# Scores of two attention items in one block of every second slot, with the product with v between their main parts

## The chip, the cores and the metric

The kernel runs on one core of a Trainium2 chip. A core has five engines that run side by side, each in its own order: TensorE (PE, with its weight loads PEld), VectorE (DVE), ScalarE (ACT), GpSimd (POOL) and SyncE (SP). The metric is the device time of one execution in microseconds (us), the median of three runs.

## The reference

Attention that keeps the 32 largest scores of each row, and then a two-layer MLP with an exact GELU on its output:

```python
batch, n_heads, seq, head_dim = (8, 8, 576, 64)
scores = (1/sqrt(D)) * (q @ k.T)                 # per batch and head
kth    = np.partition(scores, -32)[..., -32]     # 32nd largest of each row
scores = np.where(scores >= kth, scores, -1e9)
attn   = exp(scores - max); attn = attn / (sum(attn) + 1e-9)
out    = attn @ v
x = out.transpose(0, 2, 1, 3).reshape(4608, 512)
g = gelu(x @ w_in)                               # w_in 512 x 2048
return g @ w_out                                 # w_out 2048 x 512
```

Everything is in fp32. Each fp32 matmul is two passes on TensorE, so the profile counts two for each one in the code; its transposes are one pass.

## The kernel before

*Items.* Two heads make a pair (four pairs in a batch, 32 in all). An item is 128 rows of the score matrix for both heads of a pair, 2 x 576 columns in an SBUF tile `s` of which there are five. A main item `(pair, t)` with t from 0 to 3 is one block of 128 query rows. The last 64 rows of four heads (two pairs) are packed into one last item, t = 4 (`NM`). There are 144 items: in a batch 16 main ones, which go through the pairs with t even and odd next to each other, and two last ones. In batches of even number the last items come behind the main ones, in those of odd number ahead of them, so that four last items stand side by side in every 36.

*Slots.* The order of every engine is written out by hand in one loop over slots n (148 of them, some 10 to 12 us each). Slot n works on several items at once: scores of item n+2 (`scores`, TensorE and ScalarE), top 32 of item n (`top_k`, VectorE), softmax of item n-1 (ScalarE, in two halves), normalising of item n-1 (`normalise`, two GpSimd multiplies of 1.72 us), transposes of the probabilities of item n-2 (`transposes`: `tails`, which writes `tp_t`, and two of `main`, which write `tp`), and the product with v for item n-3 (`attend`, tile `o`). A product is made only for main items of odd t, for both row blocks at once, and for every last item. Main items of odd t have odd numbers, so products of main items fall into even slots; those of last items fall into two even and two odd slots.

*Scores.* The scores against the last 64 keys and against the first 512 are made apart. The last keys (`t_ps`, L280) use the full array, 128 rows of which half hold zeros in the keys' block, or 64-column tiles for last items (L294). The main scores (`s_ps`, L284, L305) use half the array's rows for each of the two heads, so that two matmuls run at once. The product with v (L448, L459) uses half the array's columns for each head. `s_ps` takes two PSUM banks and has one buffer; `t_ps`, `o`, `tp_t`, `tp` and the transposed q and k (`tp_qk`, L239) share the tag `tp` with two. ScalarE copies both parts of the scores into `s` and scales them (L288, L289).

*MLP.* Between the steps of a slot stand pieces of the MLP, one by one (`mlp(1)`): eight pieces a slot, each two matmuls or so of the first layer (`h_ps`, L500) or the second (`y_ps`, L536), as soon as their tokens are done. ScalarE's GELUs (L511) are issued in pairs at a few places (`run_gelus`), most of them at the end of a slot, and each pair costs a table load (L511) and one back to exp (L371).

*Who waits for whom.* Within a slot ScalarE's second softmax half stands behind the copies of `tp_t` and of the first `tp`. It gives the denominator (`den`, GpSimd L363), then VectorE's reciprocal (`rden`, L357), which stands behind the last max of `top_k(n)`, then GpSimd's `threshold(n)` (`neg`, `bias`) and the two multiplies of `normalise(n-1)` (L382). In the next slot TensorE's `tp_t` (L399, L404) waits for those multiplies.

The order around the scores in a slot is this:

```python
scores(n + 2)
product = attend(n - 3)
late = n > START
mlp(1)
tr = transposes(n - 2)
...
softmax(n - 1, 0)
mlp(1)
```

Where no MLP piece can go on before the product of this slot, `tp_t` is issued directly behind the product, and the tokens are set free at that place.

Of the kernel before, what the change touches and what calls it, by code (L numbers as in the profile page):

```python
# [14 lines left out]
def kernel(  # L15
# [19 lines left out]
    nc = tc.nc  # L35
    f32, i32, u32 = mybir.dt.float32, mybir.dt.int32, mybir.dt.uint32
    bf16, i16, u16 = mybir.dt.bfloat16, mybir.dt.int16, mybir.dt.uint16
    AF = mybir.ActivationFunctionType
    ALU = mybir.AluOpType

    B, H, S, D = q.shape
    P = 128
# [4 lines left out]
    NM = S // P  # L47
    SM = NM * P
    TL = S - SM
# [6 lines left out]
    scale = 1.0 / float(D) ** 0.5  # L56
# [4 lines left out]
    work = ctx.enter_context(tc.tile_pool(name="work", bufs=2))  # L61
    ps = ctx.enter_context(tc.tile_pool(name="ps", bufs=2, space=bass.MemoryType.PSUM))
# [21 lines left out]
    def raw_of(n, pair):  # L84
        return raws[n][pair % len(raws[n])]
# [120 lines left out]
    items, starts = [], []  # L206
# [14 lines left out]
    N = len(items)  # L221


    KT = SM + 2 * P
    qk_of = {}
# [26 lines left out]
    S_of, stat_of = {}, {}  # L252

    def row(i, e):
        return S_of[i][:, e * S : (e + 1) * S]

    def spread(t, step, n):

        return bass.AP(tensor=t.tensor, offset=t.offset, ap=[list(t.ap[0]), [step, 2], [1, n]])

    def half(r, e):


        return slice((r ^ e) * TL, ((r ^ e) + 1) * TL)
# [2 lines left out]

        return spread(t[:, e * TL :], step + (TL if e == 0 else -TL), TL)

    def scores(i):  # L270
        if i >= N:
            return
        pair, t = items[i]
        S_of[i] = s = work.tile([P, 2 * S], f32, tag="s", bufs=5, name="s")
        s_ps = ps.tile([P, 2, 512], f32, tag="s", bufs=1, name="s_ps")
        t_ps = ps.tile([P, 512], f32, tag="tp", name="t_ps")
        if t < NM:
            qk = qk_of[pair]
            lhsT = qk[:, t * P : (t + 1) * P]
            nc.tensor.matmul(t_ps[:, 0:P], lhsT=lhsT, rhs=qk[:, SM + P : KT], start=True, stop=True)  # L280
            for c in range(2):
                for e in range(2):
                    rows = slice(e * D, (e + 1) * D)
                    nc.tensor.matmul(  # L284
                        s_ps[:, e, c * 256 : (c + 1) * 256], lhsT=lhsT[rows, :],
                        rhs=qk[rows, KT + c * 256 : KT + (c + 1) * 256], start=True, stop=True,
                    )
            nc.scalar.activation(spread(s, S + TL, SM), s_ps, func=AF.Copy, scale=scale)  # L288
            nc.scalar.activation(s[:, SM : S + TL], t_ps[:, 0:P], func=AF.Copy, scale=scale)  # L289
        else:  # L290
            for r in range(2):
                qk = qk_of[pair + r]
                for e in range(2):
                    nc.tensor.matmul(  # L294
                        t_ps[half(r, e), r * TL : (r + 1) * TL],
                        lhsT=qk[:, SM + e * TL : SM + (e + 1) * TL],
                        rhs=qk[:, SM + P + e * TL : SM + P + (e + 1) * TL],
                        start=True, stop=True,
                    )

            for r in range(2):
                qk = qk_of[pair + r]
                for e in range(2):
                    rows = slice(e * D, (e + 1) * D)
                    nc.tensor.matmul(  # L305
                        s_ps[half(r, e), r, :], lhsT=qk[rows, SM + e * TL : SM + (e + 1) * TL],
                        rhs=qk[rows, KT:], start=True, stop=True,
                    )
            s2 = s.rearrange("p (r n) -> p r n", r=2)
            nc.scalar.activation(s2[:, :, 0:SM], s_ps, func=AF.Copy, scale=scale)  # L310
            nc.scalar.activation(
                s2[:, :, SM:S], t_ps[:, 0:P].rearrange("p (r n) -> p r n", r=2),
                func=AF.Copy, scale=scale,
            )

    def top_k(i, hooks):

# [47 lines left out]
    def softmax(i, e):  # L365

        if i < 0 or i >= N:
            return
        st, s = stat_of[i], row(i, e)
        nc.scalar.activation(s, s, func=AF.Prelu, bias=st["neg"][:, e, 1:2], scale=1.0, alpha=STEEP)  # L370
        nc.scalar.activation(  # L371
            s, s, func=AF.Exp, bias=st["bias"][:, e : e + 1], scale=1.0,
            accum_out=st["den"][:, e : e + 1],
        )
# [13 lines left out]
    def transposes(i):  # L388
# [36 lines left out]

        return [tails] + [lambda e=e: main(e) for e in range(2)]

    n_tok, read = [0], [0]

    def attend(i):  # L430

        if i < 0 or i >= N:
            return False
        pair, t = items[i]
        b, at = divmod(pair, NP)
        if t < NM and t % 2 == 0:
            return False
        pt = pt_now[0]
        o = ps.tile([P, 512], f32, tag="tp", name="o")
        n, row = (2 * P, (t - 1) * P) if t < NM else (TL, SM)  # L440
        tok = place_of(b, row)
        assert read[0] >= tok + n - RING
        c = slice(tok % RING, tok % RING + n)
        if t < NM:
            vt = raw_of("v", pair)
            for j in range(NJ):
                for e in range(2):
                    nc.tensor.matmul(  # L448
                        o[e * D : (e + 1) * D, 0:n], lhsT=vt[:, j, e, :],
                        rhs=pt[:, e * NM + j if j < NM else 2 * NM, :],  # L450
                        start=(j == 0), stop=(j == NJ - 1),
                    )
            nc.scalar.copy(out=xT[:, at, c], in_=o[:, 0:n])
        else:
            for r in range(2):
                vt = raw_of("v", pair + r)
                for j in range(NJ):
                    for e in range(2):
                        nc.tensor.matmul(  # L459
                            o[e * D : (e + 1) * D, r * TL : (r + 1) * TL], lhsT=vt[:, j, e, :],  # L460
                            rhs=pt[:, r, j, half(r, e)], start=(j == 0), stop=(j == NJ - 1),
                        )
            nc.scalar.copy(
                out=xT[:, at : at + 2, c],
                in_=o[:, 0 : 2 * TL].rearrange("p (r n) -> p r n", r=2),
            )

        if t == (NM if b % 2 == 0 else NM - 1):
            for r in range(2 if t == NM else 1):
                load("v", pair + r + NP + 1)  # L470
        if at == (NP - 1 if t < NM else NP - 2):
            assert n_tok[0] == tok
            n_tok[0] = tok + n
        return True

# [98 lines left out]
    def mlp(n):  # L576
        for _ in range(n):
            if done[0] >= len(pieces) or pieces[done[0]][0] > ready[0] or left[0] == 0:
                return
            pieces[done[0]][1]()  # L580
            done[0] += 1
            left[0] -= 1
# [18 lines left out]
    for pair in range(2):  # L601
        for piece in transpose_qk(pair, pair == 0):
            piece()
        if pair == 0:
            scores(0)
            scores(1)

# [6 lines left out]
    for pair in range(2, n_pairs):  # L616
        b, p = divmod(pair, NP)
# [3 lines left out]
    for n in range(ahead):  # L621

        left[0] = 7 if START < n < START + 2 * NP else 8
        weights_add(unit_in(n))
        scores(n + 2)
        product = attend(n - 3)
        late = n > START
        mlp(1)
        tr = transposes(n - 2)
        if product and n > START and done[0] < len(pieces) and pieces[done[0]][0] > ready[0]:  # L630

            for piece in tr[:1]:
                piece()
            tr, ready[0] = tr[1:], n_tok[0]
        softmax(n - 1, 0)
        mlp(1)
        if not late:
            softmax(n - 1, 1)
        mlp(1)
        prep = prep_in.pop(n, [])  # L640
        if len(prep) > 1 and len(tr) == 3:
            tr, prep = tr[:1] + prep[:1] + tr[1:], prep[1:]
        for piece in tr[:-1]:
            piece()
            ready[0] = n_tok[0]
            mlp(1)
        ready[0] = n_tok[0]
        if late:
            softmax(n - 1, 1)
        add_small(n - 1)  # L650
        for piece in tr[-1:] + prep:
            piece()
            mlp(1)

        run_gelus()
        mlp(left[0])
        run_gelus()
        if n < N:
            top_k(n, {3: lambda: inverse(n - 1)})
        else:  # L660
            inverse(n - 1)
        threshold(n)
        normalise(n - 1)

        weights_sign(unit_in(n))
        weights_size(unit_in(n + 1))
        if n >= FIRST:
            load_weights(n + 2)
        if n <= NP:
            load("v", n)  # L670
# [38 lines left out]
```

## Time and profile before

| | |
|---|---|
| median of 3 runs | 1660.15 us (1660.02 to 1661.66) |
| span in the profile | 1658.1 us |
| PE, DVE, ACT, POOL busy | 96%, 86%, 71%, 40% |
| scores of last keys, L280: passes, mean | 256, 289 ns |
| main scores, L284: passes, mean | 1024, 417 ns (pairs run at once) |
| product with v, L448: passes, mean | 1280, 389 ns (pairs run at once) |
| copy of the main scores, L288 | 128 x 1027 ns |
| copy of the last keys' scores, L289 | 128 x 277 ns |
| POOL multiply, L382 | 288 x 1723 ns |

A mean duration of a matmul is from its start to its modelled end, and matmuls overlap; what a block costs is read from the start of one block to the start of the next. The waits in the trace are listed by who waited for whom. PE's longest are `tp_t` for POOL (40.2 us in 11 places, nearly all of it in the first 160 us), and ACT's are for `s_ps` (144.8 us in 79 places) and `tp` (103.4 us in 121), which says that ACT is mostly ahead of PE at these places.

### The profile page before, as it was taken

How to read it: one execution, taken by the hardware profiler on the slowest of the kernel's cores; microseconds unless marked ns; L12 is line 12 of the kernel's file. 1: busy time of each engine (PE TensorE's matmuls, PEld its weight loads, DVE VectorE, ACT ScalarE, POOL GpSimd, SP SyncE). 2: the span in 40 equal slices, each digit the busy share in tenths (PEclk: the TensorE clock that was granted, in tenths of full speed). 3: DMA queues.
4: the chain of work that ended last, by engine and by line, in shares of the span. 5: the costliest groups of instructions: out<-in, count | busy, mean ns of one | idle time of the engine just before them, and what ended most of it. 6: DMA issues, size and time to landing. Idle time of an engine off the chain costs nothing.

```text
span 1658.1 us, 25071 instructions
## 1 busy us (share of the span) xinstructions
PE 1590.1 (96%) x8832; PEld 1079.1 (65%) x8832; DVE 1428.5 (86%) x3043; ACT 1182.8 (71%) x2131; POOL 661.6 (40%) x761
## 2 busy tenths in 40 slices
PE   6559999999999999999999999999999999999999
PEld 4336566766666667676666667676666666666665
DVE  7999899998999898998999888998889898999800
ACT  6888777777777777777777777777777777777720
POOL 3769653333333333333333333333333333333300
PEclk7779999999999999999999999999999999999999
DMA  6422210011100111001110111001110001000000
GB/s 162 138 99 97 84 49 1 14 29 29 37 14 22 29 30 35 1 28 36 29 28 1 43 29 43 1 14 28 44 35 1 27 15 32 5 14 3 5 13 13
DMA packets 126621, 56.14 MB, mean 34 GB/s; under 512 B 117760, under 2 KB 117792, under 8 KB 126496
## 3 DMA queue, kind: packets, MB, share of 16 engines
q1 hardware_dynamic: 125376, 54.25, 12.2%
q8 instruction: 70, 1.15, 0.3%
q14 instruction: 55, 0.45, 0.1%
q10 hardware_dynamic: 1056, 0.26, 0.1%
q0 software_dynamic: 64, 0.03, 0.0%
HBM read 45.08 MB, written 9.44 MB: 33 GB/s over the span
## 4 chain that ended last, share of the span: by engine, by line
PE 89%; DVE 6%; ACT 2%; POOL 1%; issue 1%; POOLq 0%; ACTq 0%
PE h_ps L500 30%; PE y_ps L536 29%; PE o L448 8%; PE s_ps L284 7%; PE tp L417 7%; DVE top L331 3%; DVE rest L334 3%; PE tp_qk L239 2%; PE t_ps L280 2%; PE o L459 1%; PE tp_t L399 1%; PE s_ps L305 1%; POOL s L382 1%; DVE w_in_sb L199 0%; ACT s L371 0%
## 5 line engine op out<-in xcount | busy, mean ns | idle before, releaser
L331 DVE MAX8 top<-rest 128x8 f32<-128x576 f32 x864 | 609.9, 748 | 0.0
L500 PE MATMUL h_ps<-xT,w_in_sb 128*128 128x256 f32 (+1 forms) x2560 | 554.5, 361 | 3.7 <-ACT g L511 3.7
L536 PE MATMUL y_ps<-w_out_sb,g 128*128 128x512 f32 x1152 | 549.4, 599 | 0.0
L382 POOL TENSOR_SCALAR s<-s,rden 128x576 f32<-128x576 f32 x288 | 493.5, 1723 | 1.0 <-issue 0.7
L500 PEld LDWEIGHTS h_ps<-xT,w_in_sb 128*128 128x128 f32 x2560 | 429.2, 191 | 66.7 <-issue 16.8
L334 DVE MATCH_REPLACE8 rest<-top,rest 128x576 f32<-128x576 f32 x576 | 423.7, 744 | 0.0
L363 POOL TENSOR_SCALAR den<-den 128x2 f32<-128x2 f32 x144 | 32.0, 222 | 831.7 <-ACT s L371 830.7
L536 PEld LDWEIGHTS y_ps<-w_out_sb,g 128*128 128x128 f32 x1152 | 195.0, 190 | 166.4 <-issue 164.3
L288 ACT ACTIVATE s<-s_ps 128x1024 f32<-128x1024 f32 x128 | 131.5, 1027 | 166.5 <-PE s_ps L284 144.8
L371 ACT ACTIVATE s<-s,bias 128x576 f32<-128x576 f32 x288 | 223.3, 775 | 13.0 <-ACT s L370 0.4
L370 ACT ACTIVATE s<-s,neg 128x576 f32<-128x576 f32 x288 | 224.0, 778 | 0.5 <-POOL neg L346 0.4
L424 ACT COPY pt<-tp 128x512 f32<-128x512 f32 x256 | 147.1, 575 | 103.6 <-PE tp L417 103.4
L334 DVE MATCH_REPLACE8 rest<-top,s 128x576 f32<-128x576 f32 x288 | 211.9, 744 | 0.0
L417 PEld LDWEIGHTS tp<-ident,s 128*128 128x128 f32 x1152 | 147.9, 145 | 89.3 <-issue 59.2
L331 DVE MAX8 top<-s 128x8 f32<-128x576 f32 x288 | 201.9, 743 | 3.9 <-ACT s L289 3.9
L417 PE MATMUL tp<-ident,s 128*128 128x128 f32 x1152 | 177.9, 279 | 4.3 <-ACT pt L400 4.2
L448 PE MATMUL o<-pt,raw_v 128*64 128x256 f32 x1280 | 155.1, 389 | 0.0
L284 PE MATMUL s_ps<-qk 64*128 64x256 f32 x1024 | 151.8, 417 | 0.7 <-ACT s L288 0.7
L357 DVE RECIPROCAL rden<-den 128x2 f32<-128x2 f32 x144 | 23.2, 161 | 139.9 <-POOL den L363 139.3
L448 PEld LDWEIGHTS o<-pt,raw_v 128*64 128x64 f32 x1280 | 87.5, 139 | 65.8 <-issue 23.9
L284 PEld LDWEIGHTS s_ps<-qk 64*128 64x128 f32 x1024 | 91.8, 194 | 23.7 <-issue 1.8
L511 ACT ACTIVATE g<-h_ps 128x512 f32<-128x512 f32 x144 | 78.6, 595 | 34.0 <-PE h_ps L500 33.2
(63 smaller groups left out, 1070.2 us busy)
## 6 DMA issues: line engine op xcount, KB each, us to landing
raw_q<-in_q_dram SPq DMA_DIRECT2D x64, 128.0 KB, 2.3
raw_v<-in_v_dram SPq DMA_DIRECT2D x64, 128.0 KB, 2.4
out_dram<-y SPq DMA_DIRECT2D x32, 256.0 KB, 2.1
w_out_sb<-in_moe_w_in_dram SPq DMA_DIRECT2D x16, 511.8 KB, 4.8
raw_k<-in_k_dram SPq DMA_DIRECT2D x62, 128.0 KB, 2.4
w_out_sb<-in_moe_w_out_dram SPq DMA_DIRECT2D x10, 511.8 KB, 3.9
words<-in_moe_w_out_dram SPq DMA_DIRECT2D x6, 511.8 KB, 4.7
raw_q<-in_q_dram SPq DMA_DIRECT2D x64, 16.0 KB, 2.2
```

The source lines that it names most:

```text
L284: nc.tensor.matmul(s_ps[:, e, c * 256 : (c + 1) * 256], lhsT=lhsT[rows, :], rhs=qk[rows, KT + c * 256 : KT + (c + 1) * 256], start=True, s ...
L288: nc.scalar.activation(spread(s, S + TL, SM), s_ps, func=AF.Copy, scale=scale)
L331: nc.vector.max(st["top"][:, e, 8 * r : 8 * r + 8], cur[e])
L334: nc.vector.match_replace(rest[:, e], st["top"][:, e, 8 * r : 8 * r + 8], cur[e], LOWEST)
L370: nc.scalar.activation(s, s, func=AF.Prelu, bias=st["neg"][:, e, 1:2], scale=1.0, alpha=STEEP)
L371: nc.scalar.activation(s, s, func=AF.Exp, bias=st["bias"][:, e : e + 1], scale=1.0, accum_out=st["den"][:, e : e + 1],)
L382: nc.gpsimd.tensor_scalar(s, s, st["rden"][:, e : e + 1], None, op0=ALU.mult)
L417: nc.tensor.transpose(tp[:, j * P : (j + 1) * P], s[:, first + j * P : first + (j + 1) * P], ident)
L424: nc.scalar.copy(out=dst, in_=tp.rearrange("p (j n) -> p j n", j=NM))
L448: nc.tensor.matmul(o[e * D : (e + 1) * D, 0:n], lhsT=vt[:, j, e, :], rhs=pt[:, e * NM + j if j < NM else 2 * NM, :], start=(j == 0), stop= ...
L500: nc.tensor.matmul(h_tile(u)[:, i, :], lhsT=w_in_sb[:, ko, f * P : (f + 1) * P], rhs=xT[:, ko, c0 : c0 + n], start=(ko == 0), stop=(ko == ...
L536: nc.tensor.matmul(y_of[sub], lhsT=g_of[u][:, i, sub * P : (sub + 1) * P], rhs=w_out_sb[:, f, :], start=(f == 0), stop=(f == FT - 1),)
```

## The change

Scores are no longer made for one item in every slot. In every even slot n they are made for two, items n+1 and n+2, and in odd slots for none. Within the block, the last keys' scores of both items come first, into one PSUM tile (`t_ps[:, 0:128]` and `t_ps[:, 128:256]`), and both small copies; then the main scores of the first item and their copy; then the product with v of item n-3 (`between`); then the main scores of the second item. The copy of these (`rest`) is issued on ScalarE after the first half of the softmax of item n-1. It is meant to bring matmuls that use the array in the same way together, so that TensorE changes over less often, and to use the product's time for the copy that frees `s_ps`. Before the loop only item 0 gets its scores, where it was items 0 and 1.

```diff
-    def scores(i):
+    def last_scores(i, t_ps):        # the last keys' matmuls of one item, as before
+    def main_scores(i):              # its main matmuls, as before; returns their copy
...
+        return lambda: nc.scalar.activation(dst, s_ps, func=AF.Copy, scale=scale)
+
+    def scores(ids, between=lambda: None):
+        ids = [i for i in ids if i < N]
+        if not ids:
+            between()
+            return lambda: None
+        t_ps = ps.tile([P, 512], f32, tag="tp", name="t_ps")
+        for x, i in enumerate(ids):
+            S_of[i] = work.tile([P, 2 * S], f32, tag="s", bufs=5, name="s")
+            last_scores(i, t_ps[:, x * P : (x + 1) * P])
+        for x, i in enumerate(ids):
+            ...
+            nc.scalar.activation(dst, src, func=AF.Copy, scale=scale)
+        main_scores(ids[0])()
+        between()
+        return main_scores(ids[1]) if len(ids) > 1 else lambda: None
...
+    def has_product(i):
+        return 0 <= i < N and (items[i][1] == NM or items[i][1] % 2 == 1)
...
         if pair == 0:
-            scores(0)
-            scores(1)
+            scores([0])
...
         weights_add(unit_in(n))
-        scores(n + 2)
-        product = attend(n - 3)
+        product = has_product(n - 3)
+        rest = scores([n + 1, n + 2], lambda: attend(n - 3)) if n % 2 == 0 else attend(n - 3)
         late = n > START
         mlp(1)
         tr = transposes(n - 2)
...
         softmax(n - 1, 0)
+        if n % 2 == 0:
+            rest()
         mlp(1)
```

More of the change, by code (lines that the diff above doesn't have):

```diff
@@ L268, in halves @@
         return spread(t[:, e * TL :], step + (TL if e == 0 else -TL), TL)
-    def scores(i):
-        if i >= N:
-            return
+    def last_scores(i, t_ps):
         pair, t = items[i]
-        S_of[i] = s = work.tile([P, 2 * S], f32, tag="s", bufs=5, name="s")
-        s_ps = ps.tile([P, 2, 512], f32, tag="s", bufs=1, name="s_ps")
-        t_ps = ps.tile([P, 512], f32, tag="tp", name="t_ps")
         if t < NM:
             qk = qk_of[pair]
-            lhsT = qk[:, t * P : (t + 1) * P]
-            nc.tensor.matmul(t_ps[:, 0:P], lhsT=lhsT, rhs=qk[:, SM + P : KT], start=True, stop=True)
+            nc.tensor.matmul(
+                t_ps, lhsT=qk[:, t * P : (t + 1) * P], rhs=qk[:, SM + P : KT], start=True, stop=True
+            )
+            return
+        for r in range(2):
+            qk = qk_of[pair + r]
+            for e in range(2):
+                nc.tensor.matmul(
+                    t_ps[half(r, e), r * TL : (r + 1) * TL],
+                    lhsT=qk[:, SM + e * TL : SM + (e + 1) * TL],
+                    rhs=qk[:, SM + P + e * TL : SM + P + (e + 1) * TL],
+                    start=True, stop=True,
+                )
+    def main_scores(i):
+        pair, t = items[i]
+        s = S_of[i]
+        s_ps = ps.tile([P, 2, 512], f32, tag="s", bufs=1, name="s_ps")
+        if t < NM:
+            qk = qk_of[pair]
             for c in range(2):
@@ L284, in scores @@
                     nc.tensor.matmul(
-                        s_ps[:, e, c * 256 : (c + 1) * 256], lhsT=lhsT[rows, :],
+                        s_ps[:, e, c * 256 : (c + 1) * 256], lhsT=qk[rows, t * P : (t + 1) * P],
                         rhs=qk[rows, KT + c * 256 : KT + (c + 1) * 256], start=True, stop=True,
                     )
-            nc.scalar.activation(spread(s, S + TL, SM), s_ps, func=AF.Copy, scale=scale)
-            nc.scalar.activation(s[:, SM : S + TL], t_ps[:, 0:P], func=AF.Copy, scale=scale)
-        else:
[L291 to L299, printed above, removed]
+            dst = spread(s, S + TL, SM)
+        else:
             for r in range(2):
@@ L308, in scores @@
                     )
[L309 to L314, printed above, removed]
+            dst = s.rearrange("p (r n) -> p r n", r=2)[:, :, 0:SM]
+        return lambda: nc.scalar.activation(dst, s_ps, func=AF.Copy, scale=scale)
[9 more added lines that the diff above has]
+        for x, i in enumerate(ids):
+            s, src = S_of[i], t_ps[:, x * P : (x + 1) * P]
+            if items[i][1] < NM:
+                dst = s[:, SM : S + TL]
+            else:
+                dst = s.rearrange("p (r n) -> p r n", r=2)[:, :, SM:S]
+                src = src.rearrange("p (r n) -> p r n", r=2)
+            nc.scalar.activation(dst, src, func=AF.Copy, scale=scale)
+        main_scores(ids[0])()
+        between()
+        return main_scores(ids[1]) if len(ids) > 1 else lambda: None
     def top_k(i, hooks):
@@ L426, in transposes @@
         return [tails] + [lambda e=e: main(e) for e in range(2)]
+    def has_product(i):
+        return 0 <= i < N and (items[i][1] == NM or items[i][1] % 2 == 1)
     n_tok, read = [0], [0]
     def attend(i):
-        if i < 0 or i >= N:
-            return False
+        if not has_product(i):
+            return
         pair, t = items[i]
         b, at = divmod(pair, NP)
-        if t < NM and t % 2 == 0:
-            return False
         pt = pt_now[0]
@@ L473, in attend @@
             n_tok[0] = tok + n
-        return True
     g_of, y_of, h_of = {}, {}, {}
```

## The prediction

> **What bounds the kernel now.** I read the page's busy table and chain of waits first, then the stretches, then the timelines of two neighbouring slots.
>
> ```profile
> PE 1590.1 (96%) x8832; PEld 1079.1 (65%) x8832; DVE 1428.5 (86%) x3043; ACT 1182.8 (71%) x2131; POOL 661.6 (40%) x761
> PE 89%; DVE 6%; ACT 2%; POOL 1%; issue 1%; POOLq 0%; ACTq 0%
> ```
> ```profile
> 0.00:160.00 160.00, 105.34 (x543) 74.14 (x544) 147.91 (x300) 124.30 (x202) 104.00 (x96) 0.79 0.43 128
> 160.00:1590.00 1430.00, 1421.49 (x8077) 965.32 (x8077) 1280.60 (x2744) 1051.18 (x1917) 557.62 (x666) 1.00 0.10 24
> ```
>
> The columns of the second block are the stretch, its length, then busy time of PE, PEld, DVE, ACT and POOL. VectorE sets the pace for the first 160 us (147.9 busy, PE 105.3). After that PE is busy 1421.5 of 1430 us at full clock, so only two things move the end: what PE's own stream costs, and any wait newly put into it. What else matters is how close the others follow. This is odd slot 61 and the end of even slot 60, PE's lines first, then ACT, POOL and DVE:
>
> ```profile
> 679.41 0.38 PE L280 MATMUL t_ps<-qk 128*128 128x128 f32 x2
> 679.72 1.14 PE L284 MATMUL s_ps<-qk 64*128 64x256 f32 x8
> 680.79 2.84 PE L536 MATMUL y_ps<-w_out_sb,g 128*128 128x512 f32 x6
> 683.47 0.27 PE L399 MATMUL tp_t<-ident,s 128*128 128x128 f32 x1
> ```
> ```profile
> 675.71 0.59 ACT L424 COPY pt<-tp 128x512 f32<-128x512 f32 x1 [0.75 <-PE tp L417]
> 677.69 0.19 ACT L371 ACTIVATION_READ_ACCUMULATOR s<-s,bias 128x1 f32 x1
> ```
> ```profile
> 678.75 3.42 POOL L382 TENSOR_SCALAR s<-s,rden 128x576 f32<-128x576 f32 x2
> ```
> ```profile
> 678.22 0.17 DVE L357 RECIPROCAL rden<-den 128x2 f32<-128x2 f32 x1 [1.52 <-POOL den L363]
> ```
>
> The reader is to see a chain that hangs on PE's own position in the even slot: ACT sat idle 0.75 us for the `tp` transposes, so the second softmax (ends 677.88) is tied to PE; VectorE sat idle 1.52 us for the denominator; the two normalising multiplies end at 682.17; and PE needs them at 683.47. The slack is 1.30 us, and t plus s of slot 61 (679.41 to 680.79) lies inside it. In the first slots, where PE does wait, `tp_t` starts 0.055 us after POOL ends, so the usable slack is about 1.24 us.
>
> **What the Trainium skill says.** TensorEngine Tiling (Array Packing), Key Properties: changing the tiling mode, and not just the tile, drains TensorE. The trace agrees: 128-row matmuls run at their streaming pitch (twelve h_ps matmuls to the next line 2.59 us, 0.216 each), but t_ps takes 0.314 where two pitches of 0.109 are 0.218, the product ends 0.095 after its last pitch, and s_ps 0.095 after its own. Each change of mode costs about 0.095 us. PSUM — Partial Sum Buffer, "PSUM bank collisions raise a hardware error": guard PSUM by bank; s_ps has one buffer, so new scores into it wait until ACT has read the old ones out. In the steady part of the trace they never had to, being a whole slot apart. TensorE: Matmul & The Clock Gate, the table's row on queue depth: ScalarE's queue is a strict FIFO, so a copy behind a gelu waits for it; the trace agrees below.
>
> **The change, part by part.**
> 1. *Mode changes.* Per two slots the row scores ran t→s, then t→s→product: full→row→full, full→row→column→full, five changes. Now t, t, s, product, s: four. Block by block: before 2×0.314 + 2×1.064 + 2.309 = 5.065 us, after 0.218 + 0.314 + 2×1.064 + 2.309 = 4.969, so 0.096 less. The order of the built streams has 387 changes before and 321 after. About 7 of the 66 saved fall into the VectorE-bound start and are worth nothing; 59 × 0.095 = **−5.6 us**. Column→row doesn't occur in the trace; I take the same exit (0.095) and the same row entry as from full. Lower bound 0 for the exit, upper bound twice it: ±0.1 × 65 = ±6 us. The same copies, matmuls and MLP pieces remain; moving `main_scores`' copy behind the first softmax costs ACT nothing, as ACT keeps its order and PE's even slot is longer by the same time.
>
> 2. *Odd slots lose their scores, and with them 1.378 us of cover* (0.314 + 1.064; 1.496 where the 64-key form stood, 0.095 + 0.382 + 1.019). PE reaches `tp_t` of the odd slot that much earlier after the even slot's second softmax, while softmax, denominator, reciprocal and multiplies still follow PE's unchanged place in the even slot. `tp_t` waits for POOL, and all of PE's stream, MLP included, is queued behind it. The slack (start of `tp_t` minus end of the multiplies) in the odd slots from 19 to 141, less 0.055: fifteen with 1.23 fall short by 0.146; five with 1.35 by 0.03; slots 51, 87, 123 (0.70) by 0.795; slots 53, 89, 125 (0.92) by 0.57; the rest (1.45 to 3) hold. Sum 2.19 + 0.15 + 2.39 + 1.71 = **+6.4 us**. Even slots keep their slack: relative to the even slot before, both sides stay.
>
> 3. *Start.* In slots 13, 15, 17 and 18 PE already waits for POOL or is within 0.3 us of it, and VectorE is alternately the later and the earlier. Carried through slot by slot: slot 13's wait grows from 0.58 to 1.8, which then shifts the denominators of slots 14 and 16; net +2.2 us by slot 18. Scores of item 0 are complete 0.2 us sooner, as the small copy goes first. **+2.0 us.**
>
> 4. *Second main scores wait for ACT's copy of the first.* What hides the copy (1.02 us) is the product, 2.31 us wide, or 1.315 with last rows. It hides it as long as ACT is free in time. ACT starts it after gelus and y copies that were queued at the end of the odd slot:
>
> ```profile
> 628.30 1.07 ACT L288 ACTIVATE s<-s_ps 128x1024 f32<-128x1024 f32 x1
> ```
> ```profile
> 626.12 0.38 PE L280 MATMUL t_ps<-qk 128*128 128x128 f32 x2
> 626.43 1.13 PE L284 MATMUL s_ps<-qk 64*128 64x256 f32 x8
> 627.50 1.39 PE L459 MATMUL o<-ptt,raw_v 128*64 128x64 f32 x40
> ```
>    Here (slot 56) ACT is free 2.18 us after the slot begins. Two small copies (0.16 to 0.17 each until the next starts), the large one (1.05) and 0.05 to release give 3.6; PE is through with the product at 0.53 + 1.064 + 1.315 = 2.91: 0.7 us idle, in slots 20, 56, 92, 128. In six slots (40, 48, 76, 84, 112, 120) ACT is free at 2.68, so 4.1 against 3.905: 0.2. Elsewhere it is done in time (at 2.18 with the wide product, 3.6 against 3.9). 2.8 + 1.2 = **+4.0 us**.
>
> 5. *Nine slots in which `tp_t` follows the product directly* (30, 38, 46, 66, 74, 82, 102, 110, 118; no MLP piece is ready). The second scores now stand between product and `tp_t`, whose copy ACT takes before the softmax. From the slot's start: `tp_t` copied at 5.3 to 5.45, prelu 0.86, table 1.30, exp 0.77, the moved copy 0.92, then the copy of `tp` ends at 9.85. PE's transposes of the next pair (tag `tp`, two buffers) need that buffer; they stood at 827.25 − 819.06 = 8.19 in slot 74 and now at 9.47. 0.43 × 9 = **+3.9 us**.
>
> Sum: −5.6 + 6.4 + 2.0 + 4.0 + 3.9 = +10.7, so 1670.8 us.
>
> VectorE gets no new wait: the first score copy of item n+1 stands on ACT ahead of the softmax whose denominator VectorE awaits before that item. The `s` tiles (five) free up as before.
>
> **Rivals.**
> - *Only the drains count*: all new waits are covered; 1660.15 − 5.6 = 1654.5 us, faster. For it: PE's waits in the steady part are nil now. Against it: the odd slots' slack, smaller than the cover removed, read off directly.
> - *The POOL waits come, the ACT ones don't* (ACT earlier by having no scores in odd slots): −5.6 + 8.4 = +2.8, 1663 us, within 0.2%. Against it: ACT's lateness comes from gelus tied to the odd slot's end.
> - *Column→row is the dear change*: +6 on top, 1677 us. For it: that change isn't in the trace. Against: every exit seen costs 0.095.
>
> **How the numbers follow.** Forecast as summed 0.60; only drains 0.13; POOL waits alone 0.13; dear change 0.14. Slower is the first and last, 0.74. The range goes from 1657, between the two light cases, to 1677, leaving out most of the fastest case and a tail beyond the dearest: just under 2 in 10.
>
> **What would show it.** In the changed profile: PE `tp_t` waiting for POOL about 0.15 us in many odd slots and 0.6 to 0.8 in six; s_ps waiting for ACT in ten even slots; transposes of q and k waiting for ACT's `pt` copy in nine; s→product→s blocks of 1.06, 2.31, 1.06. The forecast is wrong if odd slots show no POOL waits (then the softmax came earlier than PE's place), or if the product block before scores takes clearly over 2.31 us.

## The result, and the profile after

The changed kernel takes 1672.0 us (median of 6 runs, 1671.85 to 1673.78) against 1661.95 for the kernel before beside it: 10 us slower, ratio 1.0065 with a 95% interval of 1.0052 to 1.0078. The forecast was 1670.8. The sum was right, and all five of its terms show in the trace; but two of them were too small by about 5 us each, with opposite signs. More than half of that has one common reason, and the rest evened out by luck. That is the part to learn from.

First the busy table and the chain of waits of the changed kernel, then the long stretch after the start (length, then busy time of PE, PEld, DVE, ACT, POOL):

```profile
PE 1582.9 (95%) x8832; PEld 1069.6 (64%) x8832; DVE 1425.1 (85%) x3043; ACT 1182.1 (71%) x2131; POOL 661.9 (40%) x761
PE 75%; ACT 10%; POOL 7%; DVE 6%; issue 2%; POOLq 0%; ACTq 0%
```
```profile
160.00:1590.00 1430.00, 1409.68 (x8041) 952.47 (x8040) 1277.82 (x2744) 1046.14 (x1911) 554.65 (x663) 1.00 0.10 24
```

TensorE's 8832 passes keep it busy 7 us less in all (1582.9 against 1590.1), and still the kernel is longer. PE's share of the chain fell from 89 to 75%; ACT and POOL, 3% together, have 17%: the chain now leaves PE and goes through the softmax and the multiplies. In the long stretch PE was idle 8.5 us and is now idle 20.3.

The timeline of TensorE in slots 60 and 61, then POOL's multiplies and VectorE's reciprocal ahead of slot 61's `tp_t`:

```profile
669.51 2.74 PE L560 MATMUL y_ps<-w_out_sb,g 128*128 128x512 f32 x6
672.09 0.61 PE L275 MATMUL t_ps<-qk 128*128 128x128 f32 x4
672.63 1.13 PE L299 MATMUL s_ps<-qk 64*128 64x256 f32 x8
673.69 2.38 PE L473 MATMUL o<-pt,raw_v 128*64 128x256 f32 x20
676.00 1.14 PE L299 MATMUL s_ps<-qk 64*128 64x256 f32 x8
...
679.76 0.27 PE L423 MATMUL tp_t<-ident,s 128*128 128x128 f32 x1
...
685.07 2.74 PE L560 MATMUL y_ps<-w_out_sb,g 128*128 128x512 f32 x6
687.89 0.33 PE L423 MATMUL tp_t<-ident,s 128*128 128x128 f32 x1
```
```profile
684.41 3.42 POOL L406 TENSOR_SCALAR s<-s,rden 128x576 f32<-128x576 f32 x2
```
```profile
683.88 0.17 DVE L381 RECIPROCAL rden<-den 128x2 f32<-128x2 f32 x1 [1.64 <-POOL den L387]
```

The blocks have the lengths that were worked out: t, t 0.54, s 1.06, product 2.31, s 1.07. In slot 61 the six y_ps matmuls start at 685.07 and `tp_t` only at 687.89, 0.06 after POOL's end at 687.83. The same six take 669.51 to 672.09, 2.58 us, where nothing holds up what follows; so PE lost 0.24 us here. VectorE waited 1.64 us for the denominator, where it waited 1.52 before: it isn't what is late. Nor are the multiplies later than they were, seen from PE's place in the even slot. This is `tp_t` of slot 60 in the kernel before:

```profile
674.10 0.27 PE L399 MATMUL tp_t<-ident,s 128*128 128x128 f32 x1
```

From there to the end of the multiplies was 8.07 us (682.17), and it is 8.07 in the changed kernel (679.76 to 687.83). What has become shorter is PE's own way to the next `tp_t`.

The list of waits of the changed kernel (total, times, longest) has these:

```profile
PEld tp_t L423 <- POOL s L406: 94.8, 68, 9.1
PE s_ps L299 <- ACT s L315: 6.7, 8, 1.7
PE tp_qk L239 <- ACT pt L448: 2.9, 9, 0.3
```

PEld is TensorE's row of weight loads. Its 68 counts more than the waits, as e1 will show. The surer count goes by starts: a `tp_t` that waited starts 0.054 to 0.056 us after the end of POOL's multiplies, and one that didn't starts later than that. In the changed kernel 47 of them start so, 33 of these between slots 19 and 141, all in odd slots. In the kernel before it is 14, and none between slots 19 and 141.

### The profile page after: what moved, and what is told of

Same layout as the page of the kernel before. It is cut to its first block, busy times and chain, and to the rows that moved or that the text cites. A ratio compares the mean times of both kernels' runs of the same rounds, so it can differ in the third digit from the quotient of the medians.

```text
span 1670.1 us, 24859 instructions
## 1 busy us (share of the span) xinstructions
PE 1582.9 (95%) x8832; PEld 1069.6 (64%) x8832; DVE 1425.1 (85%) x3043; ACT 1182.1 (71%) x2131; POOL 661.9 (40%) x761
## 4 chain that ended last, share of the span: by engine, by line
PE 75%; ACT 10%; POOL 7%; DVE 6%; issue 2%; POOLq 0%; ACTq 0%
PE y_ps L560 24%; PE h_ps L524 24%; PE o L473 7%; PE s_ps L299 7%; PE tp L441 6%; POOL s L406 5%; DVE top L355 3%; DVE rest L358 3%; ACT s L395 2%; PE tp_qk L239 2%; ACT s L394 2%; PE t_ps L275 1%; PE tp_t L423 1%; ACT pt L448 1%; ACT s L315 1%
## 5 line engine op out<-in xcount | busy, mean ns | idle before, releaser
L560 PEld LDWEIGHTS y_ps<-w_out_sb,g 128*128 128x128 f32 x1152 | 200.9, 192 | 134.4 <-issue 130.6
L315 ACT ACTIVATE s<-s_ps 128x1024 f32<-128x1024 f32 x144 | 147.2, 1022 | 5.5 <-PE s_ps L299 3.1
L424 ACT COPY pt<-tp_t 128x128 f32<-128x128 f32 x128 | 33.3, 260 | 150.7 <-PE tp_t L423 150.7
```

Source lines behind the costliest of these rows:

```text
L315: return lambda: nc.scalar.activation(dst, s_ps, func=AF.Copy, scale=scale)
L560: nc.tensor.matmul(y_of[sub], lhsT=g_of[u][:, i, sub * P : (sub + 1) * P], rhs=w_out_sb[:, f, :], start=(f == 0), stop=(f == FT - 1),)
```

## The experiments

What each edit changes is shown as a diff against the changed kernel, or the kernel named. All times are set beside runs of the kernel before on the same chip (medians 1661.62 and 1661.91, within 0.3 us of the 1661.95 above, so that they are compared with the changed kernel's 1672.0 directly). Sums from traces go from `tp_t` of slot 18 to `tp_t` of slot 142, behind the start.

**e1_cover: give the odd slots their cover back.**

```diff
-        for piece in tr[:-1]:
+        cover = late and n % 2 == 1 and not product
+        if cover:
+            mlp(1)
+        for x, piece in enumerate(tr[:-1]):
             piece()
             ready[0] = n_tok[0]
-            mlp(1)
+            if x or not cover:
+                mlp(1)
```

> In odd slots without a product one MLP piece (0.86 us) moves from behind tp_t to ahead of it; nothing else moves. Theory (lost cover: tp_t comes 1.38 us sooner than the POOL multiplies allow for): the 5.9 us that the odd slots lose at tp_t in the changed kernel come back, and up to 1 us of the first slots; time 1665 to 1667, POOL waits of tp_t from slot 19 on gone. Rival (the multiplies are late because VectorE or ScalarE sets the pace): the wait moves along with tp_t's successors or shows up elsewhere, time within 1 us of 1672.

Measured: 1661.62 us, ratio to before 0.9998 (0.9990 to 1.0006). Moving one MLP piece by one place takes back the whole 10 us. Only 16 `tp_t` still start right at the end of POOL's multiplies: 13 in slots up to 18, and those of slots 51, 87 and 123, which lose 0.05 us each. The list of waits has more, and two weight loads of slot 59 show why:

```profile
PEld tp_t L423 <- POOL s L406: 59.4, 36, 9.1
```
```profile
663.62 0.19 PEld L560 LDWEIGHTS y_ps<-w_out_sb,g 128*128 128x128 f32 x1 [0.24 <-issue]
664.05 0.14 PEld L423 LDWEIGHTS tp_t<-ident,s 128*128 128x128 f32 x1 [0.24 <-POOL s L406]
```

The load of `tp_t` comes 0.24 us after the load before it, like the loads of y_ps ahead of it; that gap is no wait, though it is put down to POOL.

The wait didn't move elsewhere, so the rival falls. But the gain, 10.4 (11.2 in the traces), is well over the 5 to 7 that the theory gave: from slot 19 on, the waits of `tp_t` must have cost about 11 us, not 6. Something else must have gained 5 us that the waits had hidden; e5 finds it.

**e7_control: the same move in the kernel before.**

> On the kernel before: only the move of one MLP piece ahead of tp_t in odd slots without a product, as in e1_cover. Theory (it helps only where tp_t comes too early): no change, within 1 us of before. Rival (the move is a gain by itself, so that e1_cover shows nothing of lost cover): up to 10 us less than before.

Measured: 1660.17 us, ratio 0.9991 (0.9983 to 1.0000). In its trace, `tp_t` in slot 20 stands 1.72 us later than in the trace of the kernel before, and in slot 140 1.59: over 120 slots the move gained 0.1 us. The medians differ by 1.7 us, more than the 1 us of the theory; the traces differ by as much with the opposite sign, and single executions of the kernel before lie up to 3.5 us apart. So the trace shows no gain from the move by itself, and the interval of the medians leaves room for 2.8 us at most, not for 10; e1_cover gives back what the change had taken.

**e2_copy_later: copy the second main scores after the copy of the first `tp`, where `tp_t` follows the product directly.**

```diff
...
             tr, ready[0] = tr[1:], n_tok[0]
+            put_off = True
         softmax(n - 1, 0)
-        if n % 2 == 0:
+        if n % 2 == 0 and not put_off:
             rest()
...
         ready[0] = n_tok[0]
+        if put_off:
+            rest()
         if late:
             softmax(n - 1, 1)
```

> In the slots where tp_t follows the product directly, ScalarE copies the second main scores only after the copy of the first tp, instead of before it. Theory (the moved copy holds up the tp buffer that the next transposes of q and k need): 9 x 0.49 = 4.4 us come back, 1667.6. Rival (these transposes wait because the tails' copy waits for tp_t, whatever the scores' copy does): the wait of transposes of q and k for ScalarE stays, 1672.

Measured: 1668.25 us, ratio 1.0039 (1.0025 to 1.0052), 3.75 us less than the changed kernel. The wait of `tp_qk` for the copy of `pt` is no longer in the list. In the traces 4.9 us come back at these transposes, and 1.0 of it goes again: PE comes to `tp_t` of the odd slots earlier, and waits there in 36 places instead of 33. The place in the changed kernel is this, slot 74, TensorE and then ScalarE:

```profile
831.80 1.03 PE L524 MATMUL h_ps<-xT,w_in_sb 128*128 128x256 f32 x4
833.15 0.33 PE L239 MATMUL tp_qk<-ident,raw_q 128*128 128x128 f32 x1 [0.32 <-ACT pt L448]
```
```profile
831.62 1.00 ACT L315 ACTIVATE s<-s_ps 128x1024 f32<-128x1024 f32 x1
832.52 0.57 ACT L448 COPY pt<-tp 128x512 f32<-128x512 f32 x1
```

The four h_ps passes need 0.87, so `tp_qk` could have started at 832.67; it starts when the `pt` copy ends, at 833.1. The scores' copy stands ahead of that one for no reason: its buffer isn't needed until the next even slot.

**e3_narrow: one MLP piece between the narrow product and the second main scores.** Narrow is the product of last rows (1.315 us), wide that of main items (2.309).

```diff
         between()
+        if ids[0] % 36 == 21 and len(ids) > 1:
+            mlp(1)
         return main_scores(ids[1]) if len(ids) > 1 else lambda: None
```

> In slots 20, 56, 92 and 128 one MLP piece goes between the product and the second main scores, so that ScalarE's copy of the first is covered, at one more change of mode each. Theory: 4 x 0.73 less 4 x 0.1 to 0.2 = 2.2 to 2.5 us less, 1669.6. Rival (ScalarE is behind in these slots anyhow, so the wait moves to a later buffer): 1672.

Measured: 1671.12 us, ratio 1.0053 (1.0040 to 1.0067): 0.9 less than the changed kernel, less than was expected and within what medians of this kernel can tell. In the trace the wait is gone (all sixteen narrow products now take 1.315 us) and the kernel gains 1.6 us: 2.9 of waits less 0.8 for four more changes of mode, less about 0.4 of `tp_t` waits that became longer. What it removes is this, slot 56 of the changed kernel, TensorE and then ScalarE:

```profile
631.25 1.39 PE L484 MATMUL o<-ptt,raw_v 128*64 128x64 f32 x40
633.29 1.13 PE L299 MATMUL s_ps<-qk 64*128 64x256 f32 x8 [0.66 <-ACT s L315]
```
```profile
629.92 1.08 ACT L535 ACTIVATE g<-h_ps 128x512 f32<-128x512 f32 x2
630.89 1.08 ACT L566 COPY y<-y_ps 128x512 f32<-128x512 f32 x2
632.15 1.08 ACT L315 ACTIVATE s<-s_ps 128x1024 f32<-128x1024 f32 x1
```

Two gelus and two y copies stand ahead of the scores' copies, the last of which ends at 633.23; PE goes on at 633.29, 0.73 us after the product's 1.315.

**e4_all: the three edits together.**

> The three edits together. Theory: the gains add, 5.9 + 1 + 4.4 + 2.3 = 13.6 less than 1672, that is 1658 to 1660, which is 2 to 4 us faster than the kernel before (1662): the changes of mode saved (some 5 us) less 1.3 us of waits in six slots and 1 us of the start. Rival (fewer changes of mode gain nothing, or column to row costs as much as it saves): 1663 to 1665, no faster than before.

Measured: 1653.7 us, ratio 0.9950 (0.9937 to 0.9962): 8 us faster than before, and 18.3 faster than the changed kernel. The rival falls; fewer changes of mode do pay. (Of the three edits only e1's can be made in the kernel before as well, and e7 shows that it gains nothing there.) But the gain is 4 to 6 us more than was expected. Slot 61 here:

```profile
680.82 3.60 PE L562 MATMUL y_ps<-w_out_sb,g 128*128 128x512 f32 x8
684.25 0.27 PE L425 MATMUL tp_t<-ident,s 128*128 128x128 f32 x1
```

Eight passes in 3.43, 0.43 each, and nothing before `tp_t`.

**e5_apart: on e4_all, split the last keys' scores again.** The second item's matmuls and small copy (`last`) stand behind the product, right ahead of its main scores.

```diff
         t_ps = ps.tile([P, 512], f32, tag="tp", name="t_ps")
-        for x, i in enumerate(ids):
-            S_of[i] = work.tile([P, 2 * S], f32, tag="s", bufs=5, name="s")
-            last_scores(i, t_ps[:, x * P : (x + 1) * P])
-        for x, i in enumerate(ids):
-            s, src = S_of[i], t_ps[:, x * P : (x + 1) * P]
+        def last(x, i):
...
+        last(0, ids[0])
         main_scores(ids[0])()
         between()
...
+        if len(ids) > 1:
+            last(1, ids[1])
         return main_scores(ids[1]) if len(ids) > 1 else lambda: None
```

> On e4_all: the second item's last keys' scores stand behind the product again, right before its main scores, instead of beside the first item's. That puts one stay in the full array between column and row mode, in some 53 slots. Theory after the traces (a change of mode costs 0.095 us where a mode is left and another 0.104 on the second pass after a row mode or full mode is entered): 53 x 0.2 = 10.6 us more than e4_all's 1653.7, 1664. Theory of the prediction (0.095 in all): 53 x 0.095 = 5 more, 1658.7. Rival (modes cost nothing that isn't hidden): 1653.7.

Measured: 1663.23 us, ratio 1.0009 (1.0002 to 1.0015): 9.5 more than e4_all. That is near the theory of 0.2 us a change; 0.095 would have given 1658.7. The blocks themselves tell the two apart more surely than the total. Slot 60:

```profile
670.34 0.38 PE L275 MATMUL t_ps<-qk 128*128 128x128 f32 x2
670.66 1.13 PE L299 MATMUL s_ps<-qk 64*128 64x256 f32 x8
671.72 2.38 PE L478 MATMUL o<-pt,raw_v 128*64 128x256 f32 x20
674.03 0.49 PE L275 MATMUL t_ps<-qk 128*128 128x128 f32 x2
674.45 1.13 PE L299 MATMUL s_ps<-qk 64*128 64x256 f32 x8
```

The same two passes take 0.32 us from start to start when the full array was in use already, and 0.42 when they follow the product in column mode. Together 0.732 (from the median blocks 0.314 and 0.418), where t, t side by side take 0.538: 0.194 in 51 slots is 9.9 us. In the traces the t_ps blocks grow by just that, 9.9, while 1.9 us of waits for ACT behind the product go away and 0.4 of exits in e3's four slots: 7.5 in all. Where the other 2 us between the medians come from isn't shown.

**e6_start: on e4_all, the order of the kernel before up to slot 17.**

```diff
...
+        old = n < 18
+        if old:
+            scores([n + 2])
+            attend(n - 3)
+        elif n % 2 == 0:
+            rest = scores([n + 1, n + 2] if n > 18 else [n + 2], lambda: attend(n - 3))
+        else:
+            attend(n - 3)
...
```

> On e4_all: the order of the kernel before (one item's scores in every slot) up to slot 17, the changed order from slot 18 on. Theory (the changed order loses 1 to 3 us in the slots in which VectorE and POOL set the pace): 1651 to 1652.5. Rival (the start is VectorE's alone and doesn't mind the order): 1653.7.

Measured: 1653.33 us, ratio 0.9944 (0.9931 to 0.9958). It missed the range of the theory, and against e4_all's 1653.7, the rival's number, it decides nothing. Its trace speaks for the theory: from slot 10 to slot 18, `tp_t` moved against the kernel before by -0.15 us here, +2.5 in e4_all and +1.0 in the changed kernel. Its median is the lowest of all, by a margin that isn't shown to be more than chance.

## Why the prediction was right, by its own steps

*Changes of mode, forecast -5.6: measured -11.0, a term that was mis-sized.* I priced a change by the exit alone (0.095), and reckoned a block as ended where the next one starts. But the first full-array passes after a row or column block are slow as well: of the y_ps blocks in the kernel before, 62 between slots 18 and 142 began with a pass that took 0.533 us to the next one, against 0.430 otherwise, and 49 h_ps blocks with one that took 0.320 against 0.216 (0.213 against 0.112 for the short passes). The six y_ps matmuls in the prediction's own lines show it: 680.79 to 683.47 is 2.68, not 2.58. In the kernel before these are 111 blocks, in the changed one 57: 54 x 0.103 = 5.6 us that were not in the sum. The exits gave 52 x (0.628 - 0.538) = 4.7 between t, t and s, and 0.7 more where the form for last items or the block ahead of it is concerned: 5.4, near the forecast's 5.6. The step from column to row, the unknown of the forecast, cost nothing special: 2.309 for the product, 1.064 for the scores behind it, so the rival with a dear change falls.

*Lost cover in the odd slots, forecast +6.4: measured +11.4.* Right in kind and place: fifteen slots waited 0.25 us (forecast 0.15), three 0.90 (0.795) and three 0.68 (0.57). Between slots 19 and 141 the y_ps blocks ahead of odd `tp_t` exceed their passes by 10.4 us, of which 0.8 is the slow first pass; and a `tp_t` that had waited takes 0.164 us to the next start and not 0.109, 1.8 us more in 33 places. The forecast left out three things. PE, relieved of the slow first pass, comes to `tp_t` 0.1 us earlier still and waits as much longer, some 3 us in all. The 0.055 us after each wait make 1.8. And ahead of fourteen odd slots the multiplies end 0.9 us later, seen from `tp_t` of the even slot, than in the kernel before: the second scores' copy now stands on ACT between this `tp_t` and the second half of the softmax. The forecast had this copy cost ACT nothing. It made a wait in slot 139 alone, 0.33 us.

The net of both terms was forecast as +0.8 and came out at +0.4, though each was off by 5. In part that had to be: in a slot that waits, POOL alone sets when `tp_t` starts, so it is worth nothing there that the slow first pass has gone. But only 33 of the 62 odd slots waited, eight had the slow first pass in both kernels, and in the other 21 the missing 0.1 us was a true gain, 2.2 us. That the 0.055 us and slot 139 made up for it is luck.

*Second scores behind ACT's copy, forecast +4.0: measured 4.2.* Four narrow products were followed by 0.73 us and six wide ones by 0.21. For the narrow ones e3 shows it in the trace; the wide ones are only read off.

*Transposes of q and k behind the `pt` copy, forecast +3.9: measured 4.8,* nine times 0.48, and 0.055 after each wait. Shown by e2.

*Not in the forecast:* in eight odd slots the product of last rows now stands alone and changes the mode for itself, 8 x 0.09 = 0.7. With it, -5.4 - 5.6 + 11.4 + 4.2 + 4.8 + 0.7 = 10.1 us, and the traces differ by 1.87 us at `tp_t` of slot 18 and 11.98 at slot 142, which is 10.1.

*The start, forecast +2.0: 1.0.* Between slots 10 and 18 `tp_t` fell back by 1.0 us. The other 0.9 in the trace is there from slot 2 on. The kernel's first transposes started at 7.61 instead of 6.65, ahead of anything that the change touches, while from there to VectorE's first max it was 0.17 sooner, as forecast. Why the start lost only half of what was forecast is not shown.

The rival *only the drains count* (1654.5) falls with e1: the waits were there and cost 11 us. e4_all, with most waits gone, takes 1653.7, but that it comes so near to this rival's number is chance: a change of mode is worth twice what the rival had, and the start and six waits for ACT are still in it. The rival *POOL waits alone* falls with e2.

## What to carry to other kernels

When work is moved from one slot to another on the bounding engine, it also leaves the place where it covered somebody else's latency. List, for every wait of that engine behind the moved work, the slack in the trace, and subtract the length of what was taken away; then put other work there (here one MLP piece a slot, 10 us). And when a change of state is priced from a trace, measure from the last ordinary pass before it to the second ordinary pass after it, since a cost can sit on the far side of the block's edge.

## What the runs showed that I had not expected

A change of TensorE's tiling mode cost twice. Leaving a mode took 0.09 to 0.10 us, and the second pass after the full array or the row tiles were entered came 0.10 us late (0.05 in tiles of 64 columns, and 0.055 where the transpose `tp_t` entered the full array). A detour through the full array on the way from column to row tiles cost 0.19 us net. A `tp_t` that had stood at a semaphore started 0.055 us after the releasing POOL instruction and, in the 33 places between slots 19 and 141, took another 0.055 longer until the next could start.
